# Prologue of a fused attention and GEGLU kernel: another root in the first layer norm, a touch transfer, moved dummy matmuls

## The chip, the cores and the metric

The kernel runs on one core of one Trainium2 chip. The metric is the device time of one execution in microseconds, as the median of several runs. The core has a matrix engine (TensorE, called PE in the profile; PEld is its weight loading), a vector engine (VectorE, DVE), an activation engine (ScalarE, ACT), a general engine (GpSimd, POOL) and SyncE (SP), whose queue issues nearly all transfers between HBM and the on-chip memory SBUF. Each engine runs its own instructions in the order in which they were written, and waits on semaphores for the others. Matmul results go to eight banks of an accumulator memory called PSUM.

## The reference

One transformer layer over `x` of 2048 rows by 512 columns, float32. Layer norm without learned scale; a memory attention ("infini-attention") with 32 heads of width 16 in four segments of 512 rows; a residual; a second layer norm; a GEGLU feed-forward of width 1376; a residual. What the change touches is the first layer norm on the first 512 rows, and what stands beside it at the start:

```
def _layernorm(x, axis=-1, eps=1e-5):
    m = jnp.mean(x, axis=axis, keepdims=True)
    v = jnp.var(x, axis=axis, keepdims=True)
    return (x - m) / jnp.sqrt(v + eps)

h  = x + attention(_layernorm(x), wq, wk, wv, wo, beta)
h2 = h + geglu(_layernorm(h), w_gate, w_up, w_down)
```

Inside the attention each segment s uses `q`, `k`, `v` of its own rows for a causal softmax, and a running memory `M`, `z` of the segments before it through `phi(t) = t + 1 if t > 0 else exp(t)`.

## The kernel before, in words

Float32 products are split in two parts (a rounded high part and the rest, "hi" and "lo"), and three matmuls of the parts make one product. Work is cut into units of one column chunk (8 heads) and one segment; each unit projects q and k, moves them by transfers into stacks `stq` and `stk` in which the heads lie apart, takes the row maxima (pass a), then the exponentials and the product with v (pass b). The feed-forward follows from about the middle of the span.

The order of instructions is not written out by hand. Each piece of work is handed to a planner (`Sched`) with an engine, an estimated duration, a priority and its inputs and outputs; the planner runs through a simulated time, picks the piece that can start first (by priority among those that could start within a short window), and calls its function, which emits the instructions. So one function's instructions stand together on their engine, and the order of the calls is the order of the program. The waits are not planned: a layer below follows which tile each emitted instruction reads and writes, in the order of emission, and puts a semaphore wait on every reader for the last writer of what it reads.

What happens at the start, before the first projection:

- SP issues the first four row tiles of `x` (128 rows each, L602: `pt_111` to `pt_114` in the listings), then `wq`, `wk`, half of `wv`, then the row tiles of the second segment.
- POOL makes constants: two index tiles (L361), the identity `ident` (L381), `one` (four columns of the identity added up, L395 to L397), and zero fills of the stacks.
- DVE makes a mask `mmask` from the index tiles (L370 to L376), then the statistics of the four row tiles (L494, L495), one after the other as they land.
- The root 1/sqrt(v + eps) is worked out on DVE from integer shifts and multiplications on a tile of 128 by 4: three instructions in `g` (L505 to L511) and seven in `steps` (L518), then a bias (L542), each waiting for the one before.
- DVE normalises row tiles 1 to 3 (L536), ACT row tile 4 with the bias (L548).
- PE runs 12 dummy transposes (L500), whose results nobody reads, into one PSUM bank; then 16 transposes of the normalised row tiles (L571), by row tile, into four banks.
- ACT copies each finished bank to the hi part of `xt` (L591) and DVE takes the lo part (L592). The first projection (L634) needs the first `xt` and the split weights.
- ACT fills the first of the four K stacks with the row of ones (L422) ahead of the weights' hi parts, the second one behind the four `xt` copies, the other two later.

Of the kernel before, what the change touches and what calls it, by code (L numbers as in the profile page):

```python
# [242 lines left out]
def infini_geglu(ctx: ExitStack, tc: tile.TileContext, x, wq, wk, wv, wo, beta,  # L243
# [8 lines left out]
    def sb(name, shape, dt=F32):  # L252
        return p0.tile(shape, dt, name=name)
# [89 lines left out]
    gt = sb("gt", [P, 2, NCH])  # L343
    tick = sb("tick", [P, 1])
    aside = sb("aside", [P, D])
    o_dram = dram.tile([NSEG, 4, P, NCH, P], F32, name="o_dram")
# [10 lines left out]

    def c_iota():
        hid = vh.t[:, 0:136].rearrange("p (j e) -> p j e", e=17)
        jid = vj.t[:, 0:136].rearrange("p (j e) -> p j e", e=17)  # L360
        nc.gpsimd.iota(hid, pattern=[[0, 8], [0, 17]], base=0, channel_multiplier=1,  # L361
                       allow_small_or_imprecise_dtypes=True)
        nc.gpsimd.iota(jid, pattern=[[1, 8], [0, 17]], base=0, channel_multiplier=0,
                       allow_small_or_imprecise_dtypes=True)
    pool(1.0, -9.5, c_iota, [], [vh, vj])

    def c_mmask():
        hid, jid = vh.t[:, 0:136], vj.t[:, 0:136]
        hidi = vj.t[:, 136:272].bitcast(I32)
        nc.vector.tensor_copy(hidi, hid)  # L370
        nc.vector.tensor_scalar(hidi, hidi, 1, None, op0=OP.bitwise_and)
        nc.vector.tensor_copy(hid, hidi)
        for r in range(1, 4):
            nc.vector.tensor_scalar(jid[32 * r:32 * r + 32], jid[32 * r:32 * r + 32],
                                    -float(r % 2 + 4 * (r // 2)), None, op0=OP.add)
        nc.vector.scalar_tensor_tensor(mmask.rearrange("p j e -> p (j e)"), hid, 2.0, jid,  # L376
                                       op0=OP.mult, op1=OP.is_equal)
    dve(1000, -9.5, c_mmask, [vh, vj], [vmmask, vh, vj])

    def c_ident():  # L380
        nc.gpsimd.memset(ident, 1.0)  # L381
        nc.gpsimd.affine_select(ident, ident, pattern=[[-1, P]], compare_op=OP.is_equal, fill=0.0,
                                base=0, channel_multiplier=1)
    pool(0.5, -9, c_ident, [], [vident])

# [7 lines left out]

    def c_one():
        nc.gpsimd.tensor_tensor(one, ident[:, 3:4], ident[:, 35:36], op=OP.add)  # L395
        nc.gpsimd.tensor_tensor(one, one, ident[:, 67:68], op=OP.add)
        nc.gpsimd.tensor_tensor(one, one, ident[:, 99:100], op=OP.add)  # L397
    pool(0.7, -8.5, c_one, [vident], [vone])
    def c_fill():
# [18 lines left out]
    def c_stk(i, after):  # L418
        t = stk_t[i]
        for a in range(2):  # L420
            own, other = slice(64 * a, 64 * a + 64), slice(64 - 64 * a, 128 - 64 * a)
            act(2 * D, -4.2 + i, lambda a=a, own=own: nc.scalar.activation(  # L422
                t[own, :, a], one[own, :, None].to_broadcast([64, 2, D]), AF.Copy),
                [vone] + after, [vk0[i]], src=0.1, chain=True)
            pool(0.93, -4.2 + i, lambda a=a, other=other: nc.gpsimd.memset(
                t[other, :, a].bitcast(F32), 0.0), after, [vk0[i]], chain=True)
# [32 lines left out]
    def layer_norm(prio, rows, dst, off=False, keep=None, acq=None, done=(), behind=(), scratch=None):  # L459
        bn, mv = Val(PBN), Val(PMV)  # L460
        y = Val(PLN)

# [6 lines left out]
        def v_():  # L469
            return sc.t[:, 0:4] if scratch else v.t  # L470
# [6 lines left out]
        for t in range(4):  # L477
# [14 lines left out]
            else:  # L492
                def f(t=t):
                    nc.vector.bn_stats(bn.t[:, t], rows[t].t)  # L494
                    nc.vector.bn_aggr(mv.t[:, t], bn.t[:, t])  # L495
                dve(840, prio, f, [rows[t], *behind], [bn, mv], chain=True)
        if done and not behind:

            wm = Val(PB)
            pe(12 * 0.21, prio, lambda: [nc.tensor.transpose(  # L500
                wm.t[0:24, 0:P], bn.t.rearrange("p t k -> p (t k)"), ident) for n in range(12)],
                [bn, vident], [wm])
# [17 lines left out]
        def y_():  # L520
            return y.t
        z = Val(PLN)

        def z_():
# [8 lines left out]
        if done:  # L533
# [6 lines left out]

            def bias():
                nc.vector.scalar_tensor_tensor(b.t, m_(), -1.0, y.t, op0=OP.mult, op1=OP.mult)  # L542
            dve(3500 if behind else 3250, prio, lambda: [
                *[f() for f in [g, *[f for f, _, _ in steps], *([bias] if b else [])]],
                *[norm(t) for t in range(n)]],
                [mv, *rows, *(HL0 if behind else [])], [v, u, y, z, *([b] if b else []), *rows[:n], *done])
            if b:
                act(4, prio, lambda: nc.scalar.activation(  # L548
                    rows[3].t, rows[3].t, AF.Identity, scale=y.t[:, 3:4], bias=b.t[:, 3:4]),
                    [b, y], [rows[3]])  # L550
        else:
# [16 lines left out]
        if done and not behind:  # L568

            pts = [Val(pool_) for pool_ in ((PA, PA, PB, PD) if not behind else (PD, PD, PD, PA))]  # L570
            pe(4 * TR, prio, lambda: [nc.tensor.transpose(  # L571
                pts[dc].t[:, t * P:(t + 1) * P], rows[t].t[:, dc * P:(dc + 1) * P], ident)
                for t in range(4) for dc in range(ND)], [*rows, vident], pts, acq=dst)
            for dc in range(ND):
                split_psum(prio, pts[dc], dst[dc])
            return
# [746 lines left out]
```

## Time and profile before

| | |
|---|---|
| time, median of 3 runs | 828.93 us (828.92 to 830.05) |
| time of the profiled execution | 830.86 us |
| its span, first to last instruction | 829.0 us |
| PE busy | 808.8 us, 98% of the span |
| PEld, DVE, ACT, POOL busy | 627.4, 609.8, 563.4, 485.1 us |
| mean granted TensorE clock | 0.995 of full |

The profile is of one execution. A page gives busy time by engine, the span in 40 slices and the costliest groups of instructions. Beside it the trace answers views: the timeline (instructions in order of time, equal neighbours merged), the busy time of each engine in chosen stretches with the granted clock of TensorE, and the transfers. Matmuls are pipelined: a matmul's own duration is longer than the step from its start to the next one's, so a rate is read from the starts. The prologue, up to the first projection, is 13.4 us of the 829.0.

### The profile page before, as it was taken

The page shows a single profiled execution, that of the slowest core. Times are in us where ns is not written, and L with a number is a line of the kernel's source. Part 1 is how long each engine was busy: PE and PEld are TensorE (multiplying, and loading weights), DVE is VectorE, ACT ScalarE, POOL GpSimd, SP SyncE. Part 2 cuts the span into 40 slices and gives each one's busy share as a digit, 9 for nine tenths or more (in the row PEclk, how much of TensorE's full clock was granted, in tenths as well). Part 3 has the DMA queues.
Part 4 walks back from the last instruction along what each step waited for, and adds up shares of the span by engine and source line. Part 5 has one row for each costly group of instructions (what it writes and reads, how often), then busy time and mean ns, then how long its engine had stood idle before and what let it go on. Part 6 is the DMA issues. An engine that isn't in the chain of part 4 may idle for free.

```text
span 829.0 us, 15302 instructions
## 1 busy us (share of the span) xinstructions
PE 808.8 (98%) x4704; PEld 627.4 (76%) x4704; DVE 609.8 (74%) x1831; ACT 563.4 (68%) x1127; POOL 485.1 (59%) x719
## 2 busy tenths in 40 slices
PE   6999999999999999999989999999999999999998
PEld 4788787786867767767756688878888787888886
DVE  7889775898878778689985864666568865665665
ACT  6878788888787777876676753787467454546541
POOL 7533443444264454545746885888698676869750
PEclk9999999999999999999999899999999999999999
DMA  6543544555446555654654565531111341211202
GB/s 230 150 128 97 150 125 125 165 156 156 126 127 193 165 148 146 159 163 125 183 171 138 191 196 166 164 115 51 51 51 52 100 157 39 77 39 51 64 1 101
DMA packets 71749, 103.51 MB, mean 125 GB/s; under 512 B 14324, under 2 KB 24884, under 8 KB 71668
## 3 DMA queue, kind: packets, MB, share of 16 engines
q1 hardware_dynamic: 71668, 102.54, 42.3%
q8 instruction: 37, 0.61, 0.3%
q14 instruction: 44, 0.36, 0.2%
HBM read 54.92 MB, written 21.43 MB: 92 GB/s over the span
## 4 chain that ended last, share of the span: by engine, by line
PE 51%; ACT 2%; DVE 1%; issue 1%; POOL 1%; DMA 1%; SPq 0%; ACTq 0%; POOLq 0%
PE bank L1164 24%; PE bank L1225 14%; PE bank L992 5%; PE bank L818 2%; PE bank L919 2%; PE bank L888 2%; PE bank L622 1%; PE bank L582 1%; ACT pt L895 1%; DMA cd<-pv_dram 1%; ACT stk L1027 0%; DVE bank L1021 0%; PE bank L793 0%; POOL pt L898 0%; PE bank L881 0%
## 5 line engine op out<-in xcount | busy, mean ns | idle before, releaser
L898 POOL TENSOR_SCALAR_AFFINE_SELECT pt<-pt 128x128 f32<-128x128 f32 (+2 forms) x352 | 119.8, 348 | 173.3 <-ACT pt L895 168.8
L895 ACT ACTIVATE pt<-bank 128x512 f32<-128x512 f32 (+1 forms) x352 | 182.5, 558 | 39.6 <-PE bank L888 28.2
L826 DVE CUSTOM_DVE_ANT_0 bank<-bank,amask 128x512 f32<-128x512 f32 (+1 forms) x256 | 156.7, 637 | 32.0 <-PE bank L818 30.6
L818 PE MATMUL bank<-stk,stq 128*128 128x512 f32 (+2 forms) x384 | 130.5, 382 | 3.8 <-DVE nm L826 2.5
L888 PE MATMUL bank<-stq,stk 128*128 128x384 f32 (+2 forms) x384 | 115.1, 355 | 1.9 <-ACT pt L895 1.4
L622 PE MATMUL bank<-xt,w 128*128 128x512 f32 x360 | 102.7, 395 | 0.0
L818 PEld LDWEIGHTS bank<-stk,stq 128*128 128x128 f32 x384 | 69.3, 188 | 26.5 <-DVE nm L826 10.6
L1230 DVE TENSOR_TENSOR pt<-pt,bank 128x512 f32<-128x512 f32 x96 | 64.8, 686 | 33.3 <-PE bank L1225 33.3
L826 DVE CUSTOM_DVE_ANT_0 aside<-bank,amask 128x256 f32<-128x256 f32 (+1 forms) x256 | 76.6, 353 | 14.7 <-PE bank L818 13.4
L888 PEld LDWEIGHTS bank<-stq,stk 128*128 128x128 f32 x384 | 68.4, 190 | 21.6 <-ACT pt L895 7.3
L919 PE MATMUL bank<-pt,vaug 128*32 128x512 f32 (+3 forms) x1024 | 76.8, 436 | 0.0
L622 PEld LDWEIGHTS bank<-xt,w 128*128 128x128 f32 x360 | 65.2, 188 | 10.1 <-DVE xt L592 0.2
L919 PEld LDWEIGHTS bank<-pt,vaug 128*32 128x32 f32 x1024 | 28.7, 110 | 41.2 <-issue 33.7
L826 DVE DVE_READ_ACCUMULATOR2_ANT nm<- 128x1 f32 x512 | 57.0, 111 | 0.0
L663 PE MATMUL bank<-wv,xt 128*128 128x256 f32 x384 | 55.2, 283 | 0.0
L663 PEld LDWEIGHTS bank<-wv,xt 128*128 128x128 f32 x384 | 52.0, 189 | 1.8 <-DVE hl L705 0.2
L438 POOL TENSOR_TENSOR w<-raw,w 128x512 fp32r<-128x512 f32 x25 | 32.3, 1292 | 29.9 <-ACT w L433 21.8
L1164 PE MATMUL bank<-xt,w 128*128 128x512 f32 (+1 forms) x168 | 47.1, 399 | 0.0
L1134 POOL TENSOR_TENSOR stk<-raw,stk 128x512 fp32r<-128x512 f32 (+3 forms) x28 | 31.1, 1113 | 22.9 <-PE bank L1164 14.2
L1134 POOL TENSOR_TENSOR w<-raw,w 128x512 fp32r<-128x512 f32 (+3 forms) x34 | 39.2, 1157 | 3.9 <-ACT w L1132 3.1
L1164 PE MATMUL bank<-xt,stk 128*128 128x512 f32 (+1 forms) x138 | 38.1, 391 | 0.3 <-ACT pq L1171 0.3
L1164 PE MATMUL bank<-stk,w 128*128 128x512 f32 (+1 forms) x135 | 38.0, 391 | 0.0
(299 smaller groups left out, 1841.7 us busy)
## 6 DMA issues: line engine op xcount, KB each, us to landing
stq<-hl SPq DMA_DIRECT2D x96, 128.0 KB
stk<-hl SPq DMA_DIRECT2D x192, 64.0 KB
pv_dram<-pvs SPq DMA_DIRECT2D x32, 256.0 KB
r<-r_dram SPq DMA_DIRECT2D x28, 256.0 KB
row<-x SPq DMA_DIRECT2D x24, 256.0 KB
raw<-wg SPq DMA_DIRECT2D x20, 256.0 KB
raw<-wu SPq DMA_DIRECT2D x20, 256.0 KB
raw<-wd SPq DMA_DIRECT2D x20, 256.0 KB
```

Source lines behind the costliest of these rows:

```text
L622: nc.tensor.matmul(pm.t, w.t[:, wi, dc * P:(dc + 1) * P], XT[s][dc].t[:, xi, :], start=dc == 0 and n == 0, stop=dc == ND - 1 and n == 2)
L663: nc.tensor.matmul(pm.t[:, 256 * t:256 * t + 256], XT[s][dc].t[:, xi, t0:t0 + P], whl[wi].t[:, h, 256 * (dc % 2):256 * (dc % 2) + 256], st ...
L818: nc.tensor.matmul(sa.t[:, k * w:(k + n) * w].rearrange("x (n w) -> x n w", n=n), sq.t[:, p, i * P:(i + 1) * P], sk.t[:, p, a:a + n, 0:w], ...
L826: nc.vector.tensor_tensor_reduce(out=(sa.t if i > 1 else aside)[:, k * w:(k + 1) * w], in0=sa.t[:, k * w:(k + 1) * w], in1=amask[:, D - w: ...
L888: nc.tensor.matmul(sc.t[:, lo:lo + D - q0], sk.t[:, p, a, q0:q0 + P], sq.t[:, p, q0:D], start=True, stop=True)
L895: act(w, prio, lambda: nc.scalar.activation(e.t[:, :w], sc.t[:, :w], AF.Exp), [sc], [e])
L898: nc.gpsimd.affine_select(v, v, pattern=pat + [[1, P]], compare_op=OP.is_ge, fill=0.0, base=0, channel_multiplier=-1)
L919: nc.tensor.matmul(pv.t[32 * n:32 * n + 32, kb * P:D], va.t[:, 136 * kb + 17 * j:136 * kb + 17 * j + 32], e.t[:, lo:lo + D - kb * P], star ...
L1134: pool(0.14 + 2.13e-3 * (hi - lo), prio, lambda: nc.gpsimd.tensor_tensor(v.t[:, 1, :hi - lo], r.t[:, lo:hi], v.t[:, 0, :hi - lo].bitcast(F ...
L1164: nc.tensor.matmul(dst.t[:w], v.t[:, wi, c0 + j * w:c0 + (j + 1) * w], b[bk][j].t[:, xi, :], start=first and j == 0 and n == 0, stop=j == ...
L1225: nc.tensor.matmul(pm.t, HH[p, f, s][hi].t[:w, t * P:(t + 1) * P], v.t[:w, wi, :], start=f == fl[0] and n == 0, stop=f == fl[-1] and n == 2)
L1230: dve(D, prio, lambda a=a, pm=pm: nc.vector.tensor_tensor(a.t, a.t, pm.t, op=OP.add), [pm], [a])
```

## The change

Six edits, all ahead of the first projection or just behind it:

1. ACT issues a small transfer `touch` first: 16 columns of every eighth row of row tiles 3 and 4 of `x`, 32 rows in all. Nobody reads its result.
2. The root of the first segment's layer norm: DVE adds eps (L510 of the new kernel), ACT takes `Sqrt` of the 128 by 4 tile (L511), DVE takes the reciprocal (L557) and the bias (L558). Ten DVE instructions go. `Sqrt` lies in another of ACT's function tables than `Exp`: a tiny `Sqrt` stands at the start (L365) so that its table is loaded there, and a tiny `Exp` behind the four `xt` copies (L431), which loads the table that the kernel before loaded at its start.
3. The mask loses one cast of 128 by 136 on DVE.
4. `one` is made right behind the identity on POOL, ahead of the first zero fill of 128 by 1024.
5. ACT fills two K stacks instead of one ahead of the weights, and none behind the `xt` copies.
6. PE's dummies are 19 instead of 12, and the first of them reads the second row tile where they read the statistics before; the 16 transposes stand with row tiles 1 and 2 apart, and 3 and 4 by bank.

```
@@ -356,6 +358,11 @@
     def c_iota():
+        nc.scalar.dma_start(touch, x[2 * P:4 * P:8, 0:16])
+        nc.gpsimd.memset(ones[:, 0:1], 1.0)
+        nc.scalar.activation(ones[:, 1:2], ones[:, 0:1], AF.Sqrt)
...
@@ -369,11 +376,10 @@  c_mmask
-        nc.vector.tensor_copy(hid, hidi)
...
-        nc.vector.scalar_tensor_tensor(mmask.rearrange("p j e -> p (j e)"), hid, 2.0, jid,
+        nc.vector.scalar_tensor_tensor(mmask.rearrange("p j e -> p (j e)"), hidi, 2.0, jid,
                                        op0=OP.mult, op1=OP.is_equal)
@@ -381,6 +387,8 @@  c_ident
+        for i, r in enumerate((35, 67, 99)):
+            nc.gpsimd.tensor_tensor(one, one if i else ident[:, 3:4], ident[:, r:r + 1], op=OP.add)
...
@@ -419,9 +424,16 @@  c_stk
-            act(2 * D, -4.2 + i, lambda a=a, own=own: nc.scalar.activation(
-                t[own, :, a], one[own, :, None].to_broadcast([64, 2, D]), AF.Copy),
-                [vone] + after, [vk0[i]], src=0.1, chain=True)
+            def fill(a=a):
+
+                if i == 1:
+                    if a:
+                        nc.scalar.activation(ones[:, 1:2], ones[:, 0:1], AF.Exp)
+                    return
+                for s, b in [(i, a)] + ([(1, 0), (1, 1)] if i == 0 and a else []):
+                    rows = slice(64 * b, 64 * b + 64)
+                    nc.scalar.activation(stk_t[s][rows, :, b], one[rows, :, None].to_broadcast([64, 2, D]), AF.Copy)
+            act(2 * D, -4.2 + i, fill, [vone] + after, [vk0[i]], src=0.1, chain=True)
...
@@ -493,12 +505,17 @@  layer_norm
                 def f(t=t):
                     nc.vector.bn_stats(bn.t[:, t], rows[t].t)
                     nc.vector.bn_aggr(mv.t[:, t], bn.t[:, t])
-                dve(840, prio, f, [rows[t], *behind], [bn, mv], chain=True)
+                    if t == 3 and scratch and not behind:
+
+                        nc.vector.tensor_scalar(v_(), mv.t[:, :, 1], 1e-5, None, op0=OP.add)
+                        nc.scalar.activation(z.t, v_(), AF.Sqrt)
+                dve(840, prio, f, [rows[t], *behind], [bn, mv], chain=True,
+                    acq=[v, z] if t == 3 and scratch and not behind else [])
...
             pe(12 * 0.21, prio, lambda: [nc.tensor.transpose(
-                wm.t[0:24, 0:P], bn.t.rearrange("p t k -> p (t k)"), ident) for n in range(12)],
+                wm.t[0:24, 0:P], (ident if n else rows[1].t)[:, 0:24], ident) for n in range(19)],
                 [bn, vident], [wm])
...
@@ -538,16 +553,16 @@
-            def bias():
-                nc.vector.scalar_tensor_tensor(b.t, m_(), -1.0, y.t, op0=OP.mult, op1=OP.mult)
+            def root():
+                nc.vector.reciprocal(y.t, z.t)
+                nc.vector.scalar_tensor_tensor(b.t, mv.t[:, :, 0], -1.0, y.t, op0=OP.mult, op1=OP.mult)
+                nc.scalar.activation(rows[3].t, rows[3].t, AF.Identity, scale=y.t[:, 3:4], bias=b.t[:, 3:4])
             dve(3500 if behind else 3250, prio, lambda: [
-                *[f() for f in [g, *[f for f, _, _ in steps], *([bias] if b else [])]],
+                *[f() for f in ([g, *[f for f, _, _ in steps]] if behind else [root])],
                 *[norm(t) for t in range(n)]],
...
@@ -570,7 +585,7 @@
             pe(4 * TR, prio, lambda: [nc.tensor.transpose(
                 pts[dc].t[:, t * P:(t + 1) * P], rows[t].t[:, dc * P:(dc + 1) * P], ident)
-                for t in range(4) for dc in range(ND)], [*rows, vident], pts, acq=dst)
+                for ts in ((0,), (1,), (2, 3)) for dc in range(ND) for t in ts], [*rows, vident], pts, acq=dst)
```

Behind this stretch the order of instructions on all five engines is that of before, up to the numbers of a few tiny buffers.

On PE at the start of the program, before: the dummies write `bank_70` from the statistics `bn_153`, and the transposes of the row tiles `pt_111` to `pt_113` each begin with a wait of their own for DVE.

```order
L500 MATMUL bank_70<-ident,bn_153 24x128 [waits DVE_49,Pool_49]
L500 MATMUL bank_70<-ident,bn_153 24x128 x11
L571 MATMUL bank_68<-ident,pt_111 128x128 [waits DVE_49]
L571 MATMUL bank_69<-ident,pt_111 128x128
L571 MATMUL bank_71<-ident,pt_111 128x128
L571 MATMUL bank_65<-ident,pt_111 128x128
L571 MATMUL bank_68<-ident,pt_112 128x128 [waits DVE_49]
```

On PE in the same place, of the change:

```order
L517 MATMUL bank_70<-ident,pt_112 24x128 [waits DVE_49,Pool_49]
L517 MATMUL bank_70<-ident 24x128 x18
L586 MATMUL bank_68<-ident,pt_111 128x128
L586 MATMUL bank_69<-ident,pt_111 128x128
L586 MATMUL bank_71<-ident,pt_111 128x128
L586 MATMUL bank_65<-ident,pt_111 128x128
L586 MATMUL bank_68<-ident,pt_112 128x128
...
L586 MATMUL bank_68<-ident,pt_113 128x128 [waits DVE_49]
L586 MATMUL bank_68<-ident,pt_114 128x128 [waits Activation_49]
L586 MATMUL bank_69<-ident,pt_113 128x128
```

The first dummy now reads the row tile `pt_112` and waits for DVE, not for a transfer; the transposes of `pt_111` and `pt_112` behind the dummies have no wait of their own left.

On ACT from its first instruction to the copies of `xt`, before (`stk` are the K stacks, `w` and `wv` the weights' hi parts, `pt_114` the fourth row tile):

```order
L422 ACT_TABLE_LOAD
L422 ACTIVATE stk_87<-one 64x2x512 [waits Pool_49]
L422 ACTIVATE stk_87<-one 64x2x512
L433 ACTIVATE w_81<-raw_105 128x512 [waits DMAHW4_49]
L433 ACTIVATE w_82<-raw_106 128x512 [waits DMAHW5_49]
L451 ACTIVATE wv_85<-raw_107 128x512 [waits DMAHW6_49]
L548 ACTIVATE pt_114<-pt_114,ln_159,ln_157 128x512 [waits DMAHW3_49,DVE_49]
...
L422 ACTIVATE stk_88<-one 64x2x512 x2
```

On ACT of the change:

```order
L362 DMA touch<-x 32x16
L365 ACT_TABLE_LOAD
L365 ACTIVATE ones<-ones 128x1 [waits Pool_49]
L435 ACTIVATE stk_87<-one 64x2x512 [waits Pool_49]
L435 ACTIVATE stk_87<-one 64x2x512
L435 ACTIVATE stk_88<-one 64x2x512 x2
L511 ACTIVATE ln_157<-bank_72 128x4 [waits DVE_49]
L445 ACTIVATE w_81<-raw_105 128x512 [waits DMAHW5_49]
L559 ACTIVATE pt_114<-pt_114,ln_159,ln_158 128x512 [waits DMAHW4_49,DVE_49]
...
L431 ACT_TABLE_LOAD
L431 ACTIVATE ones<-ones 128x1 [waits Activation_49]
```

The fill of the second stack (`stk_88`) and the root (L511) stand ahead of the weights, and a second table load stands where that fill was.

## Rows read from the trace of the kernel before

**Rows 1.** The page: busy time by engine, and granted clock by slice.
```profile
PE 808.8 (98%) x4704; PEld 627.4 (76%) x4704; DVE 609.8 (74%) x1831; ACT 563.4 (68%) x1127; POOL 485.1 (59%) x719
...
PEclk9999999999999999999999899999999999999999
```

**Rows 2.** Stretches (us): length, busy time by engine, granted clock, DMA share, GB/s.
```profile
7.70:10.50 2.80, 2.73 (x13) 1.50 (x13) 2.42 (x14) 1.99 (x4) 0.00 (x0) 1.00 1.05 384
13.40:455.00 441.60, 435.42 (x3034) 327.02 (x3034) 358.52 (x1396) 348.26 (x728) 209.36 (x440) 1.00 0.52 147
458.90:465.70 6.80, 6.50 (x26) 5.11 (x29) 4.40 (x12) 4.79 (x9) 5.35 (x9) 0.50 0.25 78
```

**Rows 3.** Timeline of PE, from several windows: start, length, what, count, [idle before <-releaser].
```profile
7.70 2.72 PE L500 MATMUL bank<-ident,bn 128*24 128x128 f32 x12 [7.70 <-DVE bn L494]
...
8.94 0.84 PE L500 MATMUL bank<-ident,bn 128*24 128x128 f32 x3
...
9.58 0.63 PE L500 MATMUL bank<-ident,bn 128*24 128x128 f32 x2
...
10.49 2.58 PE L571 MATMUL bank<-ident,pt 128*128 128x128 f32 x16
...
12.03 0.49 PE L571 MATMUL bank<-ident,pt 128*128 128x128 f32 x3
...
12.36 0.49 PE L571 MATMUL bank<-ident,pt 128*128 128x128 f32 x3
...
13.43 1.42 PE L634 MATMUL bank<-xt,w 128*128 128x512 f32 x5 [0.36 <-ACT xt L591]
```

**Rows 4.** Timeline of DVE in the prologue, and a reciprocal later on.
```profile
1.95 1.19 DVE L372 CAST e<-junk 128x136 f32<-128x136 int32 x1
...
4.10 0.69 DVE L494 BATCH_NORM_STATS2 bn<-pt 128x6 f32<-128x512 f32 x1
...
6.07 0.69 DVE L494 BATCH_NORM_STATS2 bn<-pt 128x6 f32<-128x512 f32 x1 [0.27 <-DMA pt<-x]
...
6.90 0.66 DVE L494 BATCH_NORM_STATS2 bn<-pt 128x6 f32<-128x512 f32 x1
...
7.81 0.17 DVE L505 TENSOR_SCALAR bank<-mv 128x4 f32<-128x4 f32 x1
...
9.81 0.16 DVE L542 SCALAR_TENSOR_TENSOR ln<-mv,ln 128x4 f32<-128x4 f32 x1
9.89 1.45 DVE L536 TENSOR_SCALAR pt<-pt,mv,ln 128x512 f32<-128x512 f32 x3
...
19.05 0.14 DVE L486 TENSOR_SCALAR bn<-bn 128x1 f32<-128x1 f32 x1
...
42.87 0.20 DVE L1084 RECIPROCAL gt<-gt 128x8 f32<-128x8 f32 x1
```

**Rows 5.** Timeline of ACT in the prologue, and a tiny activation later on.
```profile
0.82 1.28 ACT L422 ACT_TABLE_LOAD   x1 [0.82 <-PEq L1315]
3.79 2.12 ACT L422 ACTIVATE stk<-one 64x1024 fp32r<-64x1024 f32 x2 [1.69 <-POOL one L397]
...
12.78 2.07 ACT L591 ACTIVATE xt<-bank 128x512 fp32r<-128x512 f32 x4 [1.95 <-PE bank L571]
14.71 2.12 ACT L422 ACTIVATE stk<-one 64x1024 fp32r<-64x1024 f32 x2
...
18.00 1.14 ACT L433 ACTIVATE w<-raw 128x512 fp32r<-128x512 f32 x2
19.29 0.72 ACT L489 ACTIVATE junk<-row,bn 128x512 f32<-128x512 f32 x1
...
36.05 0.20 ACT L1080 ACTIVATE gt<-gt 128x8 f32<-128x8 f32 x1
```

**Rows 6.** Timeline of POOL: the zero fill that stands ahead of `one`.
```profile
2.10 0.95 POOL L401 MEMSET stq<- 128x1024 f32 x1
```

**Rows 7.** Transfers from 0 to 20 us in 40 slices of 0.5 us: GB/s.
```profile
GB/s 0 0 0 41 111 397 389 348 254 225 303 389 373 311 311 373 365 361 393 402 406 410 410 397 406 377 295 291 102 184 266 53 197 275 25 0 0 0 0 0
```

More of the change, by code (lines that the diff above doesn't have):

```diff
@@ L344, in infini_geglu @@
     tick = sb("tick", [P, 1])
+    ones = sb("ones", [P, 2])
+    touch = sb("touch", [32, 16])
     aside = sb("aside", [P, D])
@@ L392, in infini_geglu @@
     vone, vq0, vk0, vv0 = Val(), [Val() for _ in stq_t], [Val() for _ in stk_t], [Val() for _ in va_t]
[L394 to L398, printed above, removed]
+    pool(0.7, -8.5, lambda: None, [vident], [vone])
     def c_fill():
@@ L460, in layer_norm @@
         bn, mv = Val(PBN), Val(PMV)
-        y = Val(PLN)
+        y, z = Val(PLN), Val(PLN)
         if scratch:
@@ L521, in y_ @@
             return y.t
-        z = Val(PLN)
         def z_():
@@ L547, in layer_norm @@
             if b:
-                act(4, prio, lambda: nc.scalar.activation(
-                    rows[3].t, rows[3].t, AF.Identity, scale=y.t[:, 3:4], bias=b.t[:, 3:4]),
-                    [b, y], [rows[3]])
+                act(4, prio, lambda: None, [b, y], [rows[3]])
         else:
```

## The prediction

> **What bounds the kernel now.** I read the page first: PE is busy for 808.8 of 829.0 us and no other engine above 76% [rows 1]. Then the stretches: from the first projection at 13.4 to 455 us PE is busy for 435.4 of 441.6 us [rows 2]. What the program does after its start is one dense stream on PE, so a change that moves the first projection moves the end by as much, unless another wait takes it up. All edits lie ahead of that projection or right behind it. So the sum is made on one number, the start of the first projection matmul, 13.43 [rows 3], and only the chain that leads to it counts.
>
> The timelines show that chain. DVE takes statistics of the row tiles from 4.10; the third waits for its transfer until 6.07, the fourth follows at 6.90 [rows 4]. From 7.81 to 9.81 stand ten tiny instructions, 0.20 apart, then the bias, then three normalisations from 9.89 in 1.45 us [rows 4]. PE has nothing until 7.70, runs 12 dummies, and starts the real transposes at 10.49 [rows 3], as the first normalisation ends. The copies of `xt` on ACT follow at 12.78 [rows 5], the projection at 13.43.
>
> The clock needs care. The stretch from 7.70 to 10.50 shows 1.00 in the clock column [rows 2], but the dummies there start 0.213 apart ((9.58 - 8.94) / 3), and transposes with the same 128 columns moving start 0.110 apart from 12.03 on ((12.36 - 12.03) / 3) [rows 3]. So the first stretch ran at half rate, the 1.2 GHz level, and the column has no record of it. The 16 transposes take 2.58 us [rows 3] because the first of them are still at that level.
>
> **The change part by part.**
>
> The root. Ten steps of 0.20 go. In their place: the addition of eps (0.20 to the next start), the root on ACT (0.20, by the tiny activation at 36.05 [rows 5]; 0.03 handed over, the difference of 0.20 apart and 0.17 long), the reciprocal (0.20, by the one at 42.87 [rows 4], and 0.03), and the bias, 0.08 after whose start the normalisations begin (9.81 to 9.89). That is 0.20 + 0.23 + 0.23 + 0.08 = 0.74 against 2.08: the first normalisation starts 1.34 earlier, at 8.55. ACT must be free by 8.01: its fills may start when `one` is there, 0.9 earlier than 3.79 as the 0.95 fill on POOL no longer stands ahead of it [rows 5, 6]; four fills at 2.12 for two then end at about 7.15, in time.
>
> The mask. The cast that goes took 1.19 [rows 4], and the first statistics can start that much earlier, or when row tile 1 lands. It gains nothing by itself: the third statistics wait for the transfer at 6.07 anyway. That wait is its cover, and if the transfer comes earlier the cast is what makes DVE ready for it.
>
> The touch. The transfers run at 389 GB/s around 3.25 and 5.75, and at 348, 254, 225 and 303 in the four slices between [rows 7], when row tile 3 is on its way. The dip loses (41 + 135 + 164 + 86) x 0.5 us = 213 KB, 0.55 us at 389. If the touch removes it all, statistics 3 and 4 move up by 0.55. Against that, the touch stands ahead of row tile 1, and the first two slices that move anything carry only 41 and 111 GB/s; another start like that costs up to one slice, 0.5. So the bounds are a gain of 0.55 and a loss of 0.5, and I take a gain of 0.25, since the dip is a measured row and the loss only a bound. The Trainium skill speaks against more: by "Trainium Kernel Development and Optimization", Key Constraints, transfers issued from the queues of SP, ACT and POOL share the same 16 DMA engines and interleave, so the touch doesn't run beside the rows for free. No run here shows that yet.
>
> The dummies, which decide. The listing of the new program shows that the first dummy reads the second row tile and waits for DVE, while the first eight transposes have lost their wait. No transfer is named in that wait, and the last to write that tile on DVE is its normalisation: the planner called the normalisations' function before the dummies'. So all 19 dummies, and the transposes behind them on PE, wait until the second normalisation ends. Before, that was at 10.89: the first took about 0.55 (9.89 to just ahead of 10.49), the second and third share the remaining 0.90 of the 1.45. Now it is 10.89 - 1.34 = 9.55, PE starts at 9.60, 0.05 later as before. PE has run nothing until then, as before until 7.70, so I price the dummies at the half-rate step: 19 x 0.213 = 4.05, to 13.65. Before, the first 18 or so matmuls of the program (12 dummies and about six transposes) stood at that step and the rest at 0.110, so transposes from there on are taken at 0.110. The first bank is now done with the tenth transpose, which starts 9 x 0.110 = 0.99 later, at 14.64. Before, the last of the first bank was the 13th, at 12.47 (one step after 12.36), and the projection came 0.96 behind it, through the copy on ACT. That gives 15.60. The other two normalisations, the fourth row tile on ACT and all weight parts end well ahead, under cover of the dummies. Bounds for the clock: if only 15 or 16 dummies stand at the half rate, 0.3 to 0.4 less; if all ten transposes do too, 9 x 0.103 = 0.93 more.
>
> ACT behind the copies. The fills of 2.12 at 14.71 go; a table load of 1.28 and a tiny `Exp` of 0.20 come. Before, ACT ended its last weight copy at 19.14 and then began at 19.29 what waited for DVE's statistics (19.05 + 0.14) [rows 4, 5]. DVE takes those behind the lo parts of `xt`, so they move with the projection, and ACT, 0.64 quicker, still waits for them. Nothing gained.
>
> **The sum.** 15.60 - 13.43 = 2.17 later, less 0.25 for the touch: 1.9 us later. In the profiled execution, span 829.0 and time 830.86, that makes 830.9 and 832.8. Its time lies 1.9 above the median of the runs, which carry no profiler; I put the difference on the median: 828.93 + 1.9 = 830.8.
>
> **The rivals.**
>
> *The delay shrinks to nothing measurable.* The touch gives its full 0.55 and the clock rises three dummies sooner: 2.17 - 0.55 - 0.31 = 1.3, or 830.2. For it: the dip begins where row tile 3 is due. Against: both would have to come out at their best end.
>
> *The dummies don't hold the transposes.* If the wait were met when row tile 2 lands, some time before its statistics, 19 dummies would run from about 4.5 and be over near 8.6; the three normalisations from 8.30 end by 9.75, the first bank is done at about 10.0, and the projection starts at 10.9, 2.5 earlier: 826.4, faster. It decides if PE's first matmul starts before 8.3. Against it stands the listing: a wait for DVE, and transposes without one.
>
> *The clock in the middle.* From 458.9 to 465.7 the granted clock is at half, with PE busy for 6.5 us [rows 2]. PE's gaps there may fall otherwise in a program that is shifted, and the clock stay up; that gives back half of the 6.5 at most, and I take 2.4, as part of it waits for the softmax: 828.4. For it: the profiled execution is 1.9 slower than the median, so the timed runs may not have this stretch at all; which is as well an argument against a gain.
>
> *The table loads cost more than they show.* The load is 1.28 long, but ACT's next instruction waited for `one` until 3.79 [rows 5], so up to 3.79 - 2.10 = 1.69 behind it can hide there. At 1.69 the first load ends near 4.3 (the touch's issue of up to 0.5 stands ahead), the tiny `Sqrt` at 4.5, the four fills at 8.7, and the root is 1.0 late against its input at 7.76; the second load eats the 0.64 + 0.15 of room on ACT and is 0.9 late. Together 1.9: 832.7. By the Trainium skill, "ScalarE: Activation LUTs", What ACT_TABLE_LOAD costs, a switch of tables costs the load of 1283 ns, which the row here shows, and 1380 ns of draining, which no row here shows; by that figure the two would cost 0.66 and 0.59, an estimate of 832.1.
>
> **How the numbers follow.** A difference of 0.2%, 1.7 us, is about what a measurement of this kernel tells from no change. The forecast has 58% (50 above that bound, 8 under it, as 1.9 lies close to it), the small delay 14% (within it), the dummies that hold nothing 6% (faster), the clock 8% (6 within, 2 faster), the tables 14% (slower). So slower 0.64, within 0.2% 0.28, faster 0.08. The range runs from 829.3, below the small delay, to 832.8, with the table loads and the late clock taken in; the two cases that lie below it hold 14%.
>
> **What would show it.** Right: PE's first matmul near 9.4 and not at 7.7; 19 dummies with a step of 0.213; the transposes behind 13.2 at 0.110; the first projection near 15.3; the third statistics before 6.0; DVE's root chain 0.7 long; from 25 us on the same distances as before. Wrong: dummies that start between 4 and 5; a first projection before 13.4; the root on ACT behind the fills; ACT idle behind a table load; a granted clock that is full where the dummies run, or another stretch at half rate later.

## The result, and the profile after

The changed kernel takes 832.33 us (median of nine runs, 831.07 to 835.84), the kernel before beside it 829.88 (nine runs, 827.93 to 830.35). The ratio is 1.0043, with a 95% interval of 1.0026 to 1.0060: slower, by 2.2 to 5.0 us. The prediction said slower by 1.9. The direction and the step that was said to decide came out as forecast; the size did not, for 1.9 us (0.23%) lies below the interval, and one step of the sum was wrong. One execution of one variant below took 2044 us where its eleven others took 828 to 831, and is left out of that variant's ratio.

The profiled execution of after took 835.74, one of the longest of its runs. From 28 us on, single executions drift apart by one or two us whatever the kernel (the kernel before, profiled again, had a span of 827.3 where its first had 829.0). So the two traces are compared over their first 28 us alone, where the change acts.

The page of after, busy time and granted clock; it answers to [rows 1]:

```profile
PE 810.4 (97%) x4711; PEld 627.9 (75%) x4711; DVE 609.2 (73%) x1822; ACT 565.7 (68%) x1131; POOL 485.1 (58%) x720
...
PEclk9999999999999999999999899999999999999999
```

PE's busy time is 1.6 longer with seven more matmuls, and there is still one stretch of lower clock. In the stretches of after (length, busy time by engine, granted clock, DMA share, GB/s; beside [rows 2]) it stands 5.7 later than before, as long as before:

```profile
9.40:13.50 4.10, 4.04 (x20) 2.73 (x21) 0.97 (x2) 1.00 (x2) 4.08 (x5) 1.00 1.05 402
...
15.70:455.00 439.30, 431.59 (x3000) 324.94 (x3001) 359.20 (x1396) 345.37 (x723) 203.72 (x425) 1.00 0.52 145
464.60:471.40 6.80, 6.51 (x25) 4.17 (x29) 5.45 (x8) 3.81 (x8) 4.38 (x5) 0.50 0.15 41
```

PE's timeline in after, to the first projection, and the first transposes of the second segment of 512 rows (start, length, what, count, idle time before and its releaser; beside [rows 3]):

```profile
9.46 0.37 PE L517 MATMUL bank<-ident,pt 128*24 128x128 f32 x1 [9.46 <-DVE pt L551]
9.63 4.04 PE L517 MATMUL bank<-ident 128*24 128x128 f32 x18
13.47 2.19 PE L586 MATMUL bank<-ident,pt 128*128 128x128 f32 x16
15.70 1.20 PE L649 MATMUL bank<-xt,w 128*128 128x512 f32 x4
...
28.11 1.15 PE L597 MATMUL bank<-ident,pt 128*128 128x128 f32 x3 [0.63 <-DVE pt L551]
```

PE has nothing to do until 9.46. The releaser is DVE at the normalisation's line, as the listing had said. The first projection is 2.27 later than the 13.43 of before; the second segment's transposes are 28.11 - 25.32 = 2.79 later, so 0.52 more was lost in between. DVE's timeline in after, beside [rows 4]:

```profile
2.85 0.30 DVE L382 SCALAR_TENSOR_TENSOR mmask<-junk 128x136 f32<-128x136 int32 x1
3.59 0.69 DVE L506 BATCH_NORM_STATS2 bn<-pt 128x6 f32<-128x512 f32 x1 [0.43 <-DMA pt<-x]
...
5.88 0.69 DVE L506 BATCH_NORM_STATS2 bn<-pt 128x6 f32<-128x512 f32 x1 [0.59 <-DMA pt<-x]
...
7.62 0.17 DVE L510 TENSOR_SCALAR bank<-mv 128x4 f32<-128x4 f32 x1
8.03 0.18 DVE L557 RECIPROCAL ln<-ln 128x4 f32<-128x4 f32 x1 [0.24 <-ACT ln L511]
8.24 0.16 DVE L558 SCALAR_TENSOR_TENSOR ln<-mv,ln 128x4 f32<-128x4 f32 x1
8.32 1.45 DVE L551 TENSOR_SCALAR pt<-pt,mv,ln 128x512 f32<-128x512 f32 x3
...
25.26 0.16 DVE L535 SCALAR_TENSOR_TENSOR ln<-bank,ln 128x4 f32<-128x4 f32 x1
25.46 1.12 DVE L535 SCALAR_TENSOR_TENSOR bank<-ln 128x4 f32<-128x4 f32 x1
...
27.42 1.91 DVE L551 TENSOR_SCALAR pt<-pt,mv,ln 128x512 f32<-128x512 f32 x4
```

The mask is done at 3.15, and the statistics now wait for their transfers. The root's chain takes 8.32 - 7.62 = 0.70. The last row but one stands out: a step of the second segment's root, 128 by 4 elements, takes 1.12 where its neighbours take 0.16 (and where it took 0.47 before, as shown below). The last row is that segment's four normalisations. ACT's timeline in after, beside [rows 5] (ACTq is ACT's queue issuing a transfer):

```profile
0.81 0.42 ACTq L362 DMA_DIRECT2D touch<-x  x1
1.26 1.28 ACT L365 ACT_TABLE_LOAD   x1 [1.26 <-PEq L1330]
2.55 0.20 ACT L365 ACTIVATE ones<-ones 128x1 f32<-128x1 f32 x1
3.04 4.25 ACT L435 ACTIVATE stk<-one 64x1024 fp32r<-64x1024 f32 x4 [0.28 <-POOL one L391]
7.82 0.17 ACT L511 ACTIVATE ln<-bank 128x4 f32<-128x4 f32 x1 [0.53 <-DVE bank L510]
...
15.04 2.07 ACT L606 ACTIVATE xt<-bank 128x512 fp32r<-128x512 f32 x4 [4.64 <-PE bank L586]
17.13 1.28 ACT L431 ACT_TABLE_LOAD   x1
18.42 0.20 ACT L431 ACTIVATE ones<-ones 128x1 f32<-128x1 f32 x1
...
19.15 0.62 ACT L463 ACTIVATE wv<-raw 128x512 fp32r<-128x512 f32 x1
```

ACT waits for DVE ahead of the root. The tables cost their 1.28 and nothing behind it: the next activation starts 0.01 after either load. The last row is the copy of a weight's hi part that POOL's next subtraction reads; before, it stood here:

```profile
17.48 0.61 ACT L451 ACTIVATE wv<-raw 128x512 fp32r<-128x512 f32 x1
```

This copy is 1.67 later, where the first projection is 2.27 later.

POOL's timeline in after and in before, the first of two subtractions in a row that make lo parts of weights (for after also the two as one row), and for before the slow step on DVE and the normalisations behind it:

```profile
24.00 1.30 POOL L450 TENSOR_TENSOR w<-raw,w 128x512 fp32r<-128x512 f32 x1
...
24.00 2.56 POOL L450 TENSOR_TENSOR w<-raw,w 128x512 fp32r<-128x512 f32 x2
```
```profile
22.35 1.30 POOL L438 TENSOR_TENSOR w<-raw,w 128x512 fp32r<-128x512 f32 x1
```
```profile
23.19 0.47 DVE L518 SCALAR_TENSOR_TENSOR bank<-ln 128x4 f32<-128x4 f32 x1
...
24.50 2.04 DVE L536 TENSOR_SCALAR pt<-pt,mv,ln 128x512 f32<-128x512 f32 x4
```

In before the step starts at 23.19, inside the first subtraction, and ends with it (23.66 against 23.65). In after it starts at 25.46, when the first is over and the second (to 26.56) has begun, and ends at 26.58 with the second. POOL has moved by 1.65, with ACT's copy, and DVE by 2.27, with the projection. The step is 1.12 - 0.47 = 0.65 longer and the four normalisations behind it 2.04 - 1.91 = 0.13 shorter, which makes the 0.52.

### The profile page after: what moved, and what is told of

Same layout as the page of the kernel before. It is cut to its first block, busy times and chain, and to the rows that moved or that the text cites. A ratio compares the mean times of both kernels' runs of the same rounds, so it can differ in the third digit from the quotient of the medians.

```text
span 834.0 us, 15315 instructions
## 1 busy us (share of the span) xinstructions
PE 810.4 (97%) x4711; PEld 627.9 (75%) x4711; DVE 609.2 (73%) x1822; ACT 565.7 (68%) x1131; POOL 485.1 (58%) x720
## 4 chain that ended last, share of the span: by engine, by line
PE 50%; DVE 2%; ACT 2%; DMA 1%; issue 1%; SPq 1%; POOL 0%; ACTq 0%
PE bank L1179 24%; PE bank L1240 14%; PE bank L1007 5%; PE bank L833 2%; PE bank L934 1%; PE bank L903 1%; PE bank L637 1%; ACT pt L910 1%; DMA cd<-pv_dram 1%; PE bank L597 1%; DVE row L580 0%; ACT stk L1042 0%; DVE bank L1036 0%; PE bank L808 0%; DMA stq<-amask 0%
## 5 line engine op out<-in xcount | busy, mean ns | idle before, releaser
L841 DVE CUSTOM_DVE_ANT_0 aside<-bank,amask 128x256 f32<-128x256 f32 (+1 forms) x256 | 76.6, 353 | 14.5 <-PE bank L833 13.5
```

What stands on the lines that cost most here:

```text
L841: nc.vector.tensor_tensor_reduce(out=(sa.t if i > 1 else aside)[:, k * w:(k + 1) * w], in0=sa.t[:, k * w:(k + 1) * w], in1=amask[:, D - w: ...
```

## The experiments

Three claims were tested. A: the dummies wait for DVE's second normalisation and hold the transposes, and nothing else makes the first projection later. A2, a refinement: PE is then still at the half rate, so taking dummies away again brings less than their length. C: behind the first projection, 0.5 is lost where DVE's step meets POOL's subtractions. The rivals stand in the expectations. Two positions are read in each trace, the first projection and the second segment's first transpose; "shift" is the latter against the 25.32 of before, in us and as a share of 829.9, and the ratio is against before on the same chip.

| kernel | first projection | second segment | shift | ratio (95%) |
|---|---|---|---|---|
| before | 13.43 | 25.32 | 0 | |
| before, a second time | 13.73 | 25.63 | +0.31 (0.04%) | 0.9989 (0.9972 to 1.0007) |
| after | 15.70 | 28.11 | +2.79 (0.34%) | 1.0043 (1.0026 to 1.0060) |
| before with the dummies of after | 17.00 | 28.88 | +3.56 (0.43%) | 1.0048 (1.0033 to 1.0062) |
| after with the dummies of before | 12.52 | 24.93 | -0.39 (-0.05%) | 0.9996 (0.9983 to 1.0009) |
| after with 12 dummies | 15.03 | 27.42 | +2.10 (0.25%) | 1.0032 (1.0019 to 1.0046) |
| after, squares not read twice from SBUF | 15.30 | 26.93 | +1.61 (0.19%) | 1.0027 (1.0011 to 1.0043) |
| after without the touch | 15.32 | 27.73 | +2.41 (0.29%) | 1.0035 (1.0018 to 1.0052) |
| dummies written earlier | 10.92 | 23.30 | -2.02 (-0.24%) | 0.9978 (0.9964 to 0.9993) |
| the same, squares as above | 11.11 | 23.46 | -1.86 (-0.22%) | 0.9977 (0.9960 to 0.9994) |
| after, seven `Exp` in place of one | 15.44 | 28.11 | +2.79 (0.34%) | one run, 831.38 us |
| after, four `Exp` in place of one | 15.50 | 27.47 | +2.15 (0.26%) | one run, 832.90 us |

Each shift lies inside its interval where there is one, so what is lost or won in the first 28 us can be the whole difference. It is not shown to be: in all five slower kernels the middle of the interval is 0.05 to 0.09% above the shift, which would be some half a microsecond lost further on, and no run looked for it.

**The dummies written earlier.** All of after, but the dummies are emitted with the statistics of the second row tile, so that the last writer of that tile is its transfer.

```diff
...
                     nc.vector.bn_aggr(mv.t[:, t], bn.t[:, t])
+                    if t == 1 and wm:
+                        for n in range(19):
+                            nc.tensor.transpose(wm.t[0:24, 0:P], (ident if n else rows[1].t)[:, 0:24], ident)
...
-            pe(12 * 0.21, prio, lambda: [nc.tensor.transpose(
-                wm.t[0:24, 0:P], (ident if n else rows[1].t)[:, 0:24], ident) for n in range(19)],
-                [bn, vident], [wm])
+            pe(12 * 0.21, prio, lambda: None, [bn, vident], [wm])
```

> The changed kernel, but the 19 dummies are emitted together with the statistics of the second row tile, so the first one waits for that tile's transfer and no longer for its normalisation; the order on every engine is that of the changed kernel. Theory A (the dummies' wait for the normalisation made the change slower): PE starts near 4.3 us instead of 9.5, the dummies are over near 8.4, the first projection starts near 11.0 (then bound by the weight copies on ACT that end at 10.4, plus 0.65) instead of 15.7, and the time falls by some 4.5 us against the changed kernel, to about 0.997 of the kernel before. Theory B (the loss comes from the table loads, the touch or the order on ACT, and the dummies only fill a hole): PE starts early but the first projection stays near 15, and the time stays within 1 us of the changed kernel, about 1.003 of before.

PE's timeline of this kernel:

```profile
4.44 0.37 PE L511 MATMUL bank<-ident,pt 128*24 128x128 f32 x1 [4.44 <-DMA pt<-x]
4.60 3.65 PE L511 MATMUL bank<-ident 128*24 128x128 f32 x18
8.88 2.01 PE L587 MATMUL bank<-ident,pt 128*128 128x128 f32 x16 [0.63 <-DVE pt L552]
10.92 5.81 PE L650 MATMUL bank<-xt,w 128*128 128x512 f32 x24
```

The releaser is now the transfer, the dummies end before the normalisations, and the first projection is at 10.92. The same 19 dummies, with every other part of the change in place, make the kernel 0.22% faster than before (by the ratio; the medians are 827.90 against 830.19). Claim A holds. This version beats both kernels. Its profiled execution (830.65) does not show the gain to the end: it is 2.0 ahead of before at the second segment, but its span of 828.9 is level with the 829.0 of before. So the gain rests on the twelve timed runs.

**The dummies alone, on the kernel before.**

```diff
-                wm.t[0:24, 0:P], bn.t.rearrange("p t k -> p (t k)"), ident) for n in range(12)],
+                wm.t[0:24, 0:P], (ident if n else rows[1].t)[:, 0:24], ident) for n in range(19)],
```

> The kernel before with the dummies of the change and nothing else: 19, the first reading the second row tile, emitted where they were. Theory A (the wait for the normalisation and the dummies behind it are the whole loss): PE starts at 10.94, as the second normalisation ends at 10.89; the dummies end at 15.0; the first projection starts between 16.9 and 17.4, 3.5 to 3.9 us later than before, and the time is 1.0043 to 1.0047 of before. Theory B (the dummies matter little, the other edits cost): within 0.001 of before.

PE's timeline:

```profile
10.72 0.37 PE L500 MATMUL bank<-ident,pt 128*24 128x128 f32 x1 [10.72 <-DVE pt L536]
10.89 4.00 PE L500 MATMUL bank<-ident 128*24 128x128 f32 x18
14.73 1.91 PE L571 MATMUL bank<-ident,pt 128*128 128x128 f32 x16
...
17.00 0.50 PE L634 MATMUL bank<-xt,w 128*128 128x512 f32 x1 [0.36 <-ACT xt L591]
```

Alone this edit costs 3.57 at the first projection and 0.48%, more than the whole change. The distance from there to the second segment is 11.88, as in before (11.89).

**After with the dummies of before.** The inverse edit: 12 dummies that read the statistics.

> The changed kernel with the 12 dummies of before, which read the statistics. Theory A: PE starts at 7.65, the dummies end at 10.2, the transposes follow at the half-rate step until the clock rises near 12, the first projection starts near 13.1, 0.3 before that of the kernel before: ratio 0.9995 within 0.001, so the rest of the change is worth almost nothing as long as the dummies and the cold clock stand there. Theory B: still 2 to 3 us slower than before, ratio 1.003.

PE starts at 6.98 and the first projection is at 12.52, 0.9 ahead of before and 0.6 ahead of what was expected. How much of the 0.9 the other parts of the change are worth stays open, because the third statistics started at 5.34 here, earlier than in any other trace (6.07 in before). More than half of it is lost again: DVE's step takes 1.12 here too, the second segment's transposes gain 0.39, and the ratio cannot be told from 1.

**After with 12 dummies in place of 19.**

> The changed kernel with 12 dummies instead of 19, still behind the second normalisation. If each dummy costs its own step (A1): 7 x 0.213 = 1.5 us earlier, first projection at 14.2. If the clock sets the end (A2: the granted clock rises as long after PE's start as it did, near 14.0, and the transposes run at the half-rate step until then): dummies over at 12.0, ten transposes to 14.1, first projection near 15.1, only 0.6 us earlier than with 19. Theory B: no change at all against the changed kernel.

PE's timeline:

```profile
9.67 0.37 PE L517 MATMUL bank<-ident,pt 128*24 128x128 f32 x1 [9.67 <-DVE pt L551]
9.84 2.55 PE L517 MATMUL bank<-ident 128*24 128x128 f32 x11
12.18 2.81 PE L586 MATMUL bank<-ident,pt 128*128 128x128 f32 x16
15.03 1.66 PE L649 MATMUL bank<-xt,w 128*128 128x512 f32 x6
```

Seven dummies fewer are 7 x 0.213 = 1.49, but the projection comes only 0.67 earlier. The 16 transposes take 2.81 where they take 1.91 at the full rate (the row above, of the dummies alone): (2.81 - 1.91) / 0.103, about 9 of them, ran at the half-rate step. Of the 1.49, 2.81 - 2.19 = 0.62 goes to slower transposes and 0.21 to a later start of PE (9.67, not 9.46). A2 holds.

**Squares that don't read SBUF twice.** In the second segment's root the step that is slow reads the same SBUF tile as both of its inputs. Here the value is also worked out into PSUM, by one step more, and the square reads one input from each.

```diff
...
-                 (stt(u_, z_, -10.0 / 3.0, z_, OP.add, OP.mult), [z], [u]),
+                 *([(stt(zz_, u_, 1.0, y_, OP.mult, OP.mult), [u, y], [z]),
+                    (stt(u_, zz_, -10.0 / 3.0, z_, OP.add, OP.mult), [z], [u])] if behind else
+                   [(stt(u_, z_, -10.0 / 3.0, z_, OP.add, OP.mult), [z], [u])]),
```

> The changed kernel; in the second segment's layer norm one step is computed twice, into SBUF and into PSUM, so that no step on DVE reads two SBUF tiles. In the changed kernel the step that squares took 1.12 us instead of 0.17 and ended with POOL's subtraction. Theory C (that step is held by POOL's instruction on the SBUF port they share): it takes 0.17 now, the extra step adds 0.20, and the transposes of the second segment start 0.7 earlier, near 27.4, the time falls by 0.5 to 0.7 us. Rival D (the step is slow for another reason, such as a semaphore): one of the two steps is still about 1 us long and the time rises by 0.2.

DVE's timeline, the step ahead, then the extra step and the square in one row:

```profile
24.86 0.16 DVE L535 SCALAR_TENSOR_TENSOR ln<-bank,ln 128x4 f32<-128x4 f32 x1
24.94 0.36 DVE L535 SCALAR_TENSOR_TENSOR bank<-bank,ln 128x4 f32<-128x4 f32 x2
```

Two steps in 0.36 in place of one of 1.12, and the second segment comes 26.93 - 15.30 = 11.63 behind the first projection, not 12.41. POOL's two subtractions run beside them (23.60 to 26.15). So the 1.12 was a hold and not work, and it depends on the second SBUF input. (The first projection, 0.40 earlier, is not this edit's: PE started 0.29 later, but the last dummies and all transposes ran at the full rate, 18 dummies in 3.62 and not 4.04, the transposes in 1.91 and not 2.19.)

**The same on the kernel with the early dummies.**

> The kernel with early dummies, and the squaring step of the second segment's layer norm computed so that it reads one SBUF tile and one in PSUM. Theory C (the step is held by POOL's subtraction): the step that took 0.96 takes 0.17, one step of 0.20 is added, the second segment's transposes start near 22.7 instead of 23.3, and the time is 0.6 us below that of early: about 0.997 of before, the fastest of all so far. Rival D: no gain, 0.9978 or above.

A miss. The square is quick, but the distance stays at 12.35 (12.38 without the edit). DVE's timeline and POOL's:

```profile
20.75 0.36 DVE L536 SCALAR_TENSOR_TENSOR bank<-bank,ln 128x4 f32<-128x4 f32 x2
...
21.95 2.74 DVE L557 TENSOR_SCALAR pt<-pt,mv,ln 128x512 f32<-128x512 f32 x4
```
```profile
20.49 2.54 POOL L450 TENSOR_TENSOR w<-raw,w 128x512 fp32r<-128x512 f32 x2
```

The four normalisations that follow take 2.74 (1.91 in the run before), and they start while the subtractions run until 23.03. The hold went on to the first normalisations; in the run before, they started at 26.15, when the subtractions were over, and were not held.

**After without the touch.** The line that issues it is left out.

> The changed kernel without the touch transfer. If the touch removes the dip of the transfers while row tile 3 is on its way, the third statistics start at 6.05 or later here, and the dummies 0.2 to 0.5 later than in the changed kernel (9.7 to 10.0 instead of 9.47). If it does nothing, they start anywhere between 5.3 and 6.2, as they did in four runs with the touch, and the first row tile lands a little sooner. Either way the time stays within 0.5 us of the changed kernel.

DVE's timeline, the third statistics:

```profile
5.81 0.69 DVE L505 BATCH_NORM_STATS2 bn<-pt 128x6 f32<-128x512 f32 x1 [0.61 <-DMA pt<-x]
```

They start at 5.81 without the touch and at 5.88 with it. In the eight traces with the touch they start between 5.34 and 6.17, in four without it between 5.55 and 6.07. The dip in the transfer rate also stays: in after the four slices from 3.5 us carry 348, 279, 233 and 361 GB/s (view of [rows 7]):

```profile
GB/s 0 0 0 70 66 376 414 348 279 233 361 410 385 299 336 365 303 348 381 401 410 402 401 402 406 406 393 381 291 160 328 90 0 0 0 0 0 0 0 0
```

No effect of the touch can be seen.

**The kernel before a second time.**

> The kernel before, once more, for a second profile. If the further growth of the delay from 2.8 us at 28 us to 4.9 at the end of the changed kernel's profile is a matter of single executions (short waits in the attention, a stretch at half rate that comes and goes), this profile differs from the first one of the same kernel by 1 to 2 us in the same places, while the prologue agrees within 0.3. If the growth belongs to the change, the two profiles agree within 0.3 us everywhere.

The start of one and the same kernel moves by 0.30, with its transfers (the dummies start at 7.27, not 7.70) and its clock (the 16 transposes take 3.31, not 2.58). So 0.3 in a single trace's first projection is not told from chance, and terms of this size in the sums (the touch, three matmuls more or less at the half rate) stay open.

**ScalarE slowed down.** If C's cause is ACT's 0.64 behind the copies, then ACT made slow again should take the loss away. First seven tiny `Exp` in place of one, then four.

```diff
-                        nc.scalar.activation(ones[:, 1:2], ones[:, 0:1], AF.Exp)
+                        for n in range(7):
+                            nc.scalar.activation(ones[:, 1:2], ones[:, 0:1], AF.Exp)
```

> The changed kernel with seven tiny Exp activations in place of one behind the copies of xt, so that ScalarE is about as slow there as it was with the fill (6 x 0.11 = 0.66 more). Nothing else. Theory C (GpSimd's subtractions follow ScalarE's weight copies; ScalarE became 0.64 quicker, so the subtractions fall on VectorE's squaring step): the subtractions start 0.6 to 0.7 later against the first projection, the squaring step takes about 0.5 again and not 1.12, and the second segment's first transpose comes 11.8 to 12.0 behind the first projection, as in the kernel before (11.89), though ScalarE does more work. Rival (the 12.4 of every kernel with the change comes from something else in it, the order of instructions or the new tiles): the step stays near 1.1 or the distance near 12.4, or more by ScalarE's extra work, up to 13.0. Theory A says nothing of it: first projection 15.3 to 15.8. A single look, since 0.5 us is below what the times can tell.

```profile
18.17 1.61 ACT L432 ACTIVATE ones<-ones 128x1 f32<-128x1 f32 x7
```

A miss. Seven were too many: they took 1.61, 0.23 each and not 0.11, so that ACT was late for DVE's next input too. The square took 0.72 in place of 1.12, but the distance rose to 28.11 - 15.44 = 12.67. With four:

> As the run before with four Exps in place of seven: there one took 0.23 and not 0.11, so that ScalarE came 1.4 later, more than its room of 0.74 ahead of the statistics' reader, and delayed the copies of hl itself. Three more are 3 x 0.23 = 0.70, inside that room. Theory C: the first subtraction starts 9.0 behind the first projection (8.3 in the changed kernel), VectorE's squaring step stands 9.75 behind it and takes 0.5 to 0.6, and the second segment's first transpose comes 11.8 to 12.0 behind it. Rival: 12.4 or more, as in every kernel with the change, whatever ScalarE does.

POOL's, DVE's and PE's timelines:

```profile
24.51 1.29 POOL L451 TENSOR_TENSOR w<-raw,w 128x512 fp32r<-128x512 f32 x1
```
```profile
25.25 0.57 DVE L536 SCALAR_TENSOR_TENSOR bank<-ln 128x4 f32<-128x4 f32 x1
```
```profile
15.50 1.21 PE L650 MATMUL bank<-xt,w 128*128 128x512 f32 x4
...
27.47 1.61 PE L598 MATMUL bank<-ident,pt 128*128 128x128 f32 x4 [0.19 <-DVE pt L552]
```

The step starts inside the first subtraction, ends with it (25.82 against 25.80) and takes 0.57. The distance is 27.47 - 15.50 = 11.97. More work on ACT, and PE's next segment comes 0.44 earlier: C and its cause hold. This is read from one trace; the times (single runs) cannot show 0.4 us. The traces without the change's ACT edit, at 11.88 to 11.90, point the same way.

## Why the prediction was right, and where it was wrong

**Right.** The dummies hold the transposes. PE's first matmul was forecast near 9.4 and came at 9.46; the 19 at the half-rate step took 13.47 - 9.46 = 4.01 (4.05); the root's chain 0.70 (0.74); the mask gained nothing, since the third statistics still wait for the transfer. The listing of the order was what told this: the emission of the normalisations ahead of the dummies made DVE, and not the transfer, the last writer.

**Wrong: "ACT, 0.64 quicker, still waits for them. Nothing gained", and with it "from 25 us on the same distances as before".** Not nothing, but a loss of 0.52. ACT does wait for DVE's statistics, but ahead of that wait it makes the `wv` and `w` copies that POOL's subtractions read. These came earlier against DVE, and the second subtraction instead of the first stood where DVE squares an SBUF tile. So the step that failed is the one on ACT behind the copies: it followed one consumer of ACT's work, the one with a wait, and not the other. Three `Exp` more undo most of it, 0.44 of the 0.52, and every kernel with the change that has neither slowed ACT nor the squares changed has a distance of 12.38 to 12.41, while the three traces without the change's ACT edit have 11.88 to 11.90.

By the Trainium skill, "SBUF — State Buffer", SBUF: two separate sides, a DVE operation with two SBUF inputs and a GpSimd operation that reads SBUF take turns on one pair of ports, and the one that comes second waits for the whole instruction of the other. The traces agree for this step: in place of 0.16 it took 0.47 (before), 1.12 (after), 0.72 (seven `Exp`) and 0.57 (four), by where in a subtraction of 1.3 it started, and ended each time within 0.05 of a subtraction's end; with one input from PSUM it took 0.16 again.

**Undersized: the prologue, 2.27 in place of 1.92.** Of the 0.35, 2.19 - 1.91 = 0.28 is the clock: nearly three transposes more at the half-rate step, within the bound of 0.93 that was named. The 16 transposes took 1.91 in all five other traces with 19 late dummies, so this term is one execution's and not the change's. The touch makes 0.06: it was taken at 0.25, and DVE's chain began 7.81 - 7.62 = 0.19 earlier; the experiments show no effect of the touch at all, so that 0.19 too is chance in the transfers. Another 0.09 is the second normalisation: PE starts 9.46 - 8.32 = 1.14 behind the start of the first one, where 1.05 was taken. The chain and the dummies gave back 0.04 each. Together that is 0.05 more than one kernel's start was seen to differ by.

2.27 + 0.52 = 2.79, or 0.34%, which the interval holds. Whether there is more, up to its 0.60%, the runs leave open. That 832.33 lies inside the range of 829.3 to 832.8 is in part luck: its upper end was set for table loads that cost no more than they show and for a late clock that cost 0.28, and the loss of 0.52 was not among its reasons.

**The rivals.** The dummies that hold nothing did not happen, but when they were written earlier, the first projection came at 10.92, where that rival had put it at 10.9. The table loads cost no more than they show. By the Trainium skill, "ScalarE: Activation LUTs", What ACT_TABLE_LOAD costs, 1380 ns of draining come on top of the load at a switch of tables. The trace disagrees, with the next activation 0.01 behind the load, twice, and the second load 0.02 behind the activation ahead of it (15.04 + 2.07 = 17.11, then 17.13). The half-rate stretch in the middle moved along (464.6 to 471.4) and gave nothing back.

## What to carry to other kernels

A wait is set by the last writer at the point of emission, so an instruction that is meant to run early must also be emitted ahead of whatever overwrites its input; the releaser of the first dummy (DVE or DMA) was worth 4.8 us at the first projection. When an engine off the critical path becomes quicker, follow every reader of what it writes, not only the one for which it waits. And a warm-up that starts late can stand in the way of the very work it is to speed up: 19 late dummies took 4.01 ahead of the first transpose, and taking 7 away gave back only 0.67 of their 1.49, since the transposes then ran at the half rate.

## What the runs showed of the hardware

- A step on 128 by 4 elements with both inputs in SBUF took up to 1.13 (without the touch) in place of 0.16, beside a POOL instruction that reads SBUF. A tile in PSUM as one input freed it; in one of two runs the normalisations of 128 by 512 behind it were then held (2.74 for four, 1.91 in the other).
- A stretch's granted clock of 1.00 at the start does not mean that PE ran at the full rate: the view gives 1.00 from 9.4 to 13.5 in after, where matmuls of one shape started 0.213 apart and later ones 0.110.
- Seven tiny activations in a row, each writing the same element, took 0.23 each, while one followed by another instruction held ACT for 0.11.
- A transfer of 2 KB ahead of the first rows changed neither the start of the third statistics (5.88 with it, 5.81 without) nor the dip in the rate, beyond what traces of one kernel differ by.
